# Storing an inverse transform in 16 stores of 128 partitions instead of 64 of 32, and loading the output weights in one load instead of four

## The chip, the cores and the metric

The kernel runs on one core of one Trainium2 chip. The metric is device time in microseconds (us) of one execution. The core has five engines with a queue each: PE (TensorE, matrix products into PSUM), DVE (VectorE), ACT (ScalarE), POOL (GpSimd) and SP (SyncE, which here only issues transfers). Transfers (DMAs) are issued from the SP or the POOL queue and are carried out by 16 DMA engines that the queues share.

## The reference

Two independent blocks work on 2048 positions and 640 channels each, and their results are concatenated along the channels.

- Block A is local attention with 32 heads of 20: `qkv = x @ wqkv`, each position attends to itself and 7 earlier ones (8 offsets, two apart), softmax over the 8, a weighted sum of v, then `@ wo` (640 x 640).
- Block B is a state-space convolution: a kernel K of length 2048 for each channel is summed from 192 complex exponentials, u is convolved with K through an FFT of length 4096, and `u * Dskip` is added.

```
o = einsum("bhsw,bhswd->bhsd", softmax(logits), v gathered at 8 offsets);  a = o @ wo
y = irfft(rfft(u, 4096) * rfft(K, 4096))[:2048];  b = y + u * Dskip
out = concat([a, b], axis=-1)            # (1, 2048, 1280), bf16
```

## The kernel before, in words

Everything is in bf16 with sums in PSUM. The first 270 us compute K for the five channel groups, the forward transforms, the products and the first half of the inverse transform (its results, Z, go to HBM, tensors `Zmdram` and `Zldram`), beside the projections of block A. The last 65 us, which the change touches, mix three streams:

- the weighted sum of v (`av_step`, 716): one DVE product per offset (tile `prod2` or a part of `atp`, six buffers in a ring, 714), then 16 matrix products with the identity that add it into PSUM (`ps_o`); after the eighth offset ACT copies `ps_o` into the tile `o`;
- the output product (`out_piece`, 744): five products `ps_op` of `o` and the weights `wo`, a copy into one of six `ob` rows, and a store of 128 rows of 1280 bytes;
- the second half of the inverse (`Inverse.part`, 791): 24 pieces, three for each q of 0 to 7 (blocks 0 to 2, 3 to 5 and 6 to 7 of eight). A piece is 8 or 12 matrix products of the constant table `HB` and a Z tile into `ps_ib`, and an ACT copy into the tile `ysb` (800). `ysb` has four buffers, one for each q modulo 4 (792), so the pieces of q = 4 reuse the buffer of q = 0.

When blocks 0 to 3 (half 0) or 4 to 7 (half 1) of a q are in `ysb`, they are stored: four stores of 32 partitions each, two from SP and two from POOL, 32 rows of 1280 bytes each (803, 804). Below, "store 1/0" is half 0 of q = 1. An ACT copy into a reused buffer must wait until the stores that read the blocks it overwrites have landed: the copy of blocks 3 to 5 of q = 4 waits for stores 0/0 and 0/1, the copy of blocks 0 to 2 of q = 5 waits for store 1/0.

The Z tiles are loaded by `load` (779): for q = 2 and 3 the tile lies in `LPC` and is loaded from SP by five loads of 384 KB, each of which follows the one before; for q = 6 and 7 it is loaded from POOL (and its last fifth from SP). The output weights (`open_out`, 704) are loaded from POOL into `wo`, whose place was that of the v weights until then, by four loads of 32 partitions.

The order of all instructions was worked out in advance. `Plan` (854) records each instruction, or each run of products into one PSUM tile, as a numbered group, and `issue` (889) issues the groups as the written list `ORDER` says and keeps that order on each engine. So ACT, PE, DVE and both DMA queues work strictly in order: one that waits holds up all behind it. The framework gives each DMA of the POOL queue one of eight semaphores in turn, and each DMA of the SP queue one of eight others; a DMA is issued only when the one before it on its semaphore has landed.

One more helper matters for the prediction: `hold` (391) writes the convolution table in stores from 128 partitions, whose side in HBM has an outer dimension of 8 over rows that do not join up:

```
400  dst = Kd[:, start + 256 * b:start + 256 * b + 256].rearrange("i (r s) x -> i r (s x)", s=16)
401  nc.sync.dma_start(out=dst, in_=Kh[:, b0 + b].rearrange("p s x -> p (s x)"))
```

Of the kernel before, what the change touches and what calls it, by code (L numbers as in the profile page):

```python
# [287 lines left out]
def small_half(tc, pools, co, R4, TA, TX, h):  # L288
# [22 lines left out]
    for part, sl in zip(Q, (slice(0, 16), slice(16, 48))):  # L311
        TT(part[:, 0:3:2], bc(RB[:, :, sl], 1, 2), trig[:, :, :, sl], A.mult)
# [209 lines left out]
class Attention:  # L522
# [181 lines left out]
    def open_out(self, a2):  # L704
        nc = self.nc
        self.o = a2.tile([128, 5, S], bf16, name="o")
        self.o4 = self.o[:].rearrange("p j (s i) -> p j s i", s=4)
        self.wo = self.ta.tile([128, 5, D], bf16, name="wo", tag="TX")
        wsrc = self.A_wo.rearrange("(h j dd) e -> dd h j e", j=5, dd=4)
        for dd in range(4):  # L710
            nc.gpsimd.dma_start(out=self.wo[32 * dd:32 * dd + 32], in_=wsrc[dd])
        self.ob = self.ta.tile([128, 6, D], bf16, name="ob", tag="cT")
        ring = self.ta.tile([128, 4, 2048], bf16, name="prod2", tag="R0")
        self.ring = [self.AP_[:, 2], self.AP_[:, 3]] + [ring[:, i] for i in range(4)]
# [51 lines left out]
class Inverse:  # L766
# [24 lines left out]
    def part(self, q, b0, n):  # L791
        nc = self.nc
        ysb = self.ysbs[:, q % 4]
        ps = self.att.one("ps_ib")
        for i in range(n):
            grp, g = divmod(b0 + i, 4)
            for x in range(4):
                l = 8 * q + 4 * grp + x
                self.att.MM(ps[32 * x:32 * x + 32, 160 * i:160 * i + 160], lhsT=self.HB[:, l, :], rhs=self.t[q // 2][:, g, :, l % 16, :], start=(i == 0), stop=True, skip_group_check=True, tile_position=(0, 32 * x))
        nc.scalar.copy(out=ysb[:, b0:b0 + n].rearrange("p b (t c u) -> p b c t u", c=NCH, u=4), in_=ps[:, 0:160 * n].rearrange("p (b c t u) -> p b c t u", b=n, c=NCH, u=4))  # L800
        if b0 > 0:
            grp = b0 // 6
            for x in range(4):
                (nc.sync, nc.gpsimd)[x % 2].dma_start(out=self.dst[2 * q + grp, x], in_=ysb[32 * x:32 * x + 32, 4 * grp:4 * grp + 4].rearrange("p b e -> p (b e)"))

    def parts(self):
        return [(lambda q=q, b=b, n=n: self.part(q, b, n)) for q in range(8) for b, n in ((0, 3), (3, 3), (6, 2))]
# [124 lines left out]
1086 1091-1092 1087 1155 1175 1093 1096 1149 1098 1156 1097 1151 1099 1165 1150 1147 1152-1153 1148 1178 1154 1166 1210 1170-1171 1239 1157 1186 1163 1158 1196  # L932
1195 1173 1172 1159 1182 1164 1161 1183-1185 1225 1197 1160 1240 1199 1211 1162 1198 1190 1200-1201 1212 1226 1180 1213 1176 1216 1181 1202 1189 1177 1191-1194
1229-1230 1278-1279 1222-1223 1290 1203 1217 1247 1204-1205 1291 1250-1251 1254 1233 1214 1234 1227 1215 1206 1220 1228 1260 1255 1207 1252 1265 1274 1253 1221
1261 1248 1275 1238 1271 1237 1262 1235-1236 1266 1249 1299 1276 1272 1300 1258 1273 1246 1244 1243 1280 1277 1245 1259 1224 1242 1263-1264 1256-1257 1285
1281-1283 1358 1356 1296 1359 1269-1270 1267 1357 1306 1284 1360 1303 1307 1312 1373 1315 1374 1286 1268 1308 1347 1297 1317 1304 1313 1316 1298 1305 1314 1348
1301 1326 1302 1318 1334 1310 1335 1340 1349 1352 1319 1332 1351 1350 1311 1323 1426 1294 1333 1321-1322 1292 1338-1339 1353 1361 1336 1325 1328 1354 1295
1367-1368 1345 1324 1425 1337 1309 1375 1372 1287 1376 1329 1320 1369 1547 1371 1535 1327 1377-1378 1364 1330 1341 1331 1548 1342 1379 1346 1362 1343 1370 1365
1553 1423 1393 1380 1536 1293 1355 1363 1366 1344 1382 1549 1551 1567 1550 1407 1381 1552 1554 1384 1395 1422 1383 1396 1568 1394 1288 1561 1424 1533 1427 1562
1397 1408 1398 1534 1409-1412 1571 1570 1437 1569 1564 1537-1539 1413 1566 1445 1563 1540 1430 1565 1414 1572 1421 1428 1446 1438 1429 1439 1463 1468 1454 1289  # L940
1464-1465 1460 1455 1451 1440 1466-1467 1457 1452 1441-1442 1475 1447-1448 1453 1477 1456 1476 1431 1443 1473 1478-1479 1449 1458 1432 1461 1469 1444 1450 1415
1471 1481 1474 1459 1385 1416 1480 1484 1433 1462 1436 1386 1482 1489 1435 1434 1506 1487 1490 1485 1628 1495 1488 1470 1483 1491 1629 1486 1405 1472 1503 1498
1406 1419-1420 1509 1519 1499 1417-1418 1492 1511 1510 1520 1609 1514 1512-1513 1493-1494 1497 1505 1610 1496 1504 1507 1527 1508 1516 1515 1622 1541 1518 1521
1544 1623 1528 1530 1526 1529 1522-1523 1626 1631 1517 1573 1624-1625 1558 1632 1627 1531 1542 1532 1543 1524 1545-1546 1630 1633 1555 1387 1525 1399 1589 1556
1388 1559 1574 1557 1400 1560 1575-1577 1389 1500 1392 1600 1401 1404 1403 1390-1391 1597 1501 1402 1592 1595 1502 1598 1614 1611 1596 1639 1599 1615-1616 1578
1640 1582 1619 1617-1618 1579 1588 1583 1591 1594 1602 1590 1593 1601 1634 1612 1620 1613 1621 1603 1637 1642 1604-1608 1580 1636 1638 1635 1644 1581 1643 1641
1649 1646-1647 1584-1587 1645 1650 1664 1648 1669 1651 1665 1657 1670 1667 1658 1652 1668 1671 1654 1653 1659 1655-1656 1662 1660-1661 1663 1666
"""


# [6 lines left out]
def body(tc, pools, prm, B_u, B_Dskip, Sd, Zds, Kd, LPd, A_x, A_wqkv, A_wo, out_a, out_b):  # L957
# [50 lines left out]
    def half_table(c, h, part):  # L1008
        made = trig_half(tc, pools, B, c, h, part)
        trig[c, h] = made if part == "TA" else (trig[c, h][0], made[1])  # L1010
# [240 lines left out]
```

## Time and profile before

| | |
|---|---|
| time, median of 3 runs | 368.22 us (367.98 to 368.53) |
| time of the profiled execution | 364.96 us |
| its span, first to last instruction | 363.2 us |
| granted PE clock, mean of the span | 0.911 |
| busy: PE, DVE, ACT, POOL | 297.8, 305.2, 275.9, 56.8 us |
| DMA traffic, mean over the span | 159 GB/s |

The profiled execution took 3.26 us less than the median of the three runs without a profile; 1.8 us of its time lie outside the span. In the rows of the profile, start and duration come first, in us, then the engine and what it did as `out<-in`, then in brackets how long the engine had been idle and what ended that. All instructions show line L895, since `issue` records them all there; so one goes by tiles, not by lines. "SPq" is the SP queue issuing; the number beside it is the time to issue, not to land. In a table of windows the columns are the length, the busy time and count of PE, of weight loads, DVE, ACT and POOL, then the granted PE clock, the mean busy share of the 16 DMA engines (a little over 1 where packets overlap) and what they moved.

### The profile page before, as it was taken

The page shows a single profiled execution, that of the slowest core. Times are in us where ns is not written, and L with a number is a line of the kernel's source. Part 1 is how long each engine was busy: PE and PEld are TensorE (multiplying, and loading weights), DVE is VectorE, ACT ScalarE, POOL GpSimd, SP SyncE. Part 2 cuts the span into 40 slices and gives each one's busy share as a digit, 9 for nine tenths or more (in the row PEclk, how much of TensorE's full clock was granted, in tenths as well). Part 3 has the DMA queues.
Part 4 walks back from the last instruction along what each step waited for, and adds up shares of the span by engine and source line. Part 5 has one row for each costly group of instructions (what it writes and reads, how often), then busy time and mean ns, then how long its engine had stood idle before and what let it go on. Part 6 is the DMA issues. An engine that isn't in the chain of part 4 may idle for free.

```text
span 363.2 us, 15210 instructions
## 1 busy us (share of the span) xinstructions
PE 297.8 (82%) x6737; PEld 209.4 (58%) x6747; DVE 305.2 (84%) x435; ACT 275.9 (76%) x427; POOL 56.8 (16%) x109
## 2 busy tenths in 40 slices
PE   1076886774697779788699999999999998699996
PEld 1034584533586469685376567947758764265654
DVE  5995999998899999834971997489999999689992
ACT  2999899999789999999576745938948636456752
POOL 8433200000001000000000011000002005533550
PEclk9997697698579879989899999999999999579999
DMA  6788222337646623669995375764511969993333
GB/s 143 194 226 256 57 56 52 114 115 212 176 148 155 191 63 68 209 129 219 219 184 190 81 186 154 201 243 152 205 64 40 254 189 256 264 230 111 98 120 115
DMA packets 88385, 57.57 MB, mean 159 GB/s; under 512 B 60576, under 2 KB 80480, under 8 KB 88192
## 3 DMA queue, kind: packets, MB, share of 16 engines
q1 hardware_dynamic: 83616, 44.91, 47.0%
q0 software_dynamic: 4256, 11.57, 11.6%
q8 instruction: 53, 0.87, 1.0%
q10 hardware_dynamic: 448, 0.13, 0.1%
q14 instruction: 12, 0.10, 0.1%
HBM read 27.58 MB, written 20.06 MB: 131 GB/s over the span
## 4 chain that ended last, share of the span: by engine, by line
PE 49%; ACT 10%; DVE 10%; DMA 7%; SPq 5%; issue 3%; POOL 0%; ACTq 0%; DVEq 0%
PE ps_k L895 10%; PE ps_f L895 10%; PE ps_q L895 6%; PE ps_v L895 6%; PE ps_ia L895 6%; SPq L895 5%; ACT A L895 3%; DVE prod L895 3%; PE ps_l L895 3%; PE ps_op L895 2%; PE ps_o L895 2%; ACT R L895 2%; ACT Sg L895 2%; PE ps_ph L895 2%; DMA wo<-in_A_wo_dram 2%
## 5 line engine op out<-in xcount | busy, mean ns | idle before, releaser
L895 DVE TENSOR_TENSOR Y<-G,F 128x768 bf16<-128x768 bf16 (+1 forms) x48 | 54.0, 1150 | 19.6 <-PE ps_k L895 19.6
L895 PE MATMUL ps_ph<-LPC 128*64 128x512 bf16 (+5 forms) x210 | 44.1, 412 | 20.7 <-DMA LPC<-mid 10.9
L895 ACT CAST Sg<-ps_f 128x1024 bf16<-128x1024 f32 x40 | 38.6, 1043 | 3.3 <-PE ps_f L895 3.3
L895 PEld LDWEIGHTS <-LPC 128*128 128x128 bf16 (+1 forms) x220 | 18.8, 120 | 38.7 <-issue 20.5
L895 ACT CAST A<-ps_f 128x1024 bf16<-128x1024 f32 x40 | 39.5, 1031 | 1.4 <-PE ps_f L895 1.1
L895 ACT ACTIVATE R<-LPC 128x192 bf16<-128x192 f32 (+1 forms) x105 | 36.9, 429 | 2.5 <-DVE X L895 2.3
L895 DVE TENSOR_TENSOR prod<-v,atp 128x2048 bf16<-128x2048 bf16 (+2 forms) x32 | 31.4, 1018 | 3.2 <-PE ps_o L895 3.2
L895 PEld LDWEIGHTS <-X 128*32 128x32 bf16 x1920 | 22.8, 112 | 15.4 <-issue 7.5
L895 ACT ACT_TABLE_LOAD x21 | 26.9, 1283 | 4.8 <-DMA ldt<-in_B_log_dt_dram 4.5
L895 PE MATMUL ps_k<-Y,X 128*32 128x40 bf16 x1536 | 22.4, 212 | 9.0 <-DVE X L895 3.8
L895 PE MATMUL ps_f<-A,T 128*128 128x128 bf16 x320 | 24.0, 224 | 6.0 <-ACT Sg L895 2.2
L895 ACT ACTIVATE TA<-ps_ph 128x896 bf16<-128x896 int16 x30 | 26.3, 938 | 2.8 <-PE ps_ph L895 2.7
L895 PEld LDWEIGHTS <-wv 128*32 128x32 bf16 x720 | 22.7, 120 | 7.7 <-issue 0.6
L895 DVE TENSOR_TENSOR prod<-wq,LPC 128x5120 bf16<-128x5120 bf16 (+1 forms) x11 | 20.1, 1849 | 7.2 <-ACT LPC L895 7.2
L895 DVE TENSOR_TENSOR X<-R,TX 128x768 bf16<-128x768 bf16 x40 | 21.0, 556 | 6.1 <-ACT TX L895 3.2
L895 PEld LDWEIGHTS <-T 128*128 128x128 bf16 x320 | 19.7, 100 | 9.5 <-issue 8.0
L895 PE MATMUL ps_op<-wo,o 128*128 128x320 bf16 x160 | 24.2, 302 | 0.2
L895 DVE TENSOR_TENSOR prod<-qT,LPC 128x1024 bf16<-128x1024 bf16 (+1 forms) x16 | 23.1, 1486 | 0.8 <-PE ps_l L895 0.8
L895 PE MATMUL ps_v<-xT,wv 128*32 128x512 bf16 x400 | 23.5, 380 | 0.0
L895 PE MATMUL ps_q<-xT,wq 128*128 128x512 bf16 x100 | 22.8, 379 | 0.0
L895 PE MATMUL ps_k<-xT,wk 128*128 128x512 bf16 x100 | 22.7, 379 | 0.0
L895 POOL DMA_DIRECT2D out_dram<-ysb x32 | 16.2, 511 | 36.2 <-ACT ysb L895 33.3
(129 smaller groups left out, 623.8 us busy)
## 6 DMA issues: line engine op xcount, KB each, us to landing
Zmdram<-Z SPq DMA_DIRECT2D x16, 256.0 KB
Xp<-X SPq DMA_DIRECT2D x20, 192.0 KB
Sdram<-Sg SPq DMA_DIRECT2D x12, 256.0 KB
P<-Sdram SPq DMA_DIRECT2D x6, 512.0 KB
P<-Sdram SPq DMA_DIRECT2D x12, 256.0 KB
Z<-Zmdram POOLq DMA_DIRECT2D x8, 384.0 KB, 6.5
U<-in_B_u_dram SPq DMA_DIRECT2D x4, 640.0 KB
Ksb<-Kdram SPq DMA_DIRECT2D x20, 128.0 KB
```

Of the source, the lines that this page charges most:

```text
L895: ins = getattr(getattr(self.tc.nc, engine), method)(*map(real, a), **{n: real(x) for n, x in k.items()})
```

## The change

In `Inverse.part` the four stores of a half become one store from 128 partitions; half 0 goes from SP and half 1 from POOL. In `open_out` the four loads of `wo` become one load into 128 partitions from POOL. Bytes and layout in HBM stay as they are. On the HBM side a store is now 4 x 32 rows of 640 values, where the outer 4 steps by one position and the 32 by 64 positions; the load of `wo` reads 4 x 160 rows of 640 values. On the SBUF side both have 128 partitions.

```
-        for dd in range(4):
-            nc.gpsimd.dma_start(out=self.wo[32 * dd:32 * dd + 32], in_=wsrc[dd])
+        nc.gpsimd.dma_start(out=self.wo[:], in_=wsrc)
...
             grp = b0 // 6
-            for x in range(4):
-                (nc.sync, nc.gpsimd)[x % 2].dma_start(out=self.dst[2 * q + grp, x], in_=ysb[32 * x:32 * x + 32, 4 * grp:4 * grp + 4].rearrange("p b e -> p (b e)"))
+            (nc.sync, nc.gpsimd)[grp].dma_start(out=self.dst[2 * q + grp], in_=ysb[:, 4 * grp:4 * grp + 4].rearrange("p b e -> p (b e)"))
```

There are 51 groups less (1672 before), so `ORDER` is renumbered. All other groups keep their order. Each store stands where the last of its four stood, and the load of `wo` where the third of its four stood.

More of the change, by code (lines that the diff above doesn't have):

```diff
@@ L934 @@
 1229-1230 1278-1279 1222-1223 1290 1203 1217 1247 1204-1205 1291 1250-1251 1254 1233 1214 1234 1227 1215 1206 1220 1228 1260 1255 1207 1252 1265 1274 1253 1221
-1261 1248 1275 1238 1271 1237 1262 1235-1236 1266 1249 1299 1276 1272 1300 1258 1273 1246 1244 1243 1280 1277 1245 1259 1224 1242 1263-1264 1256-1257 1285
-1281-1283 1358 1356 1296 1359 1269-1270 1267 1357 1306 1284 1360 1303 1307 1312 1373 1315 1374 1286 1268 1308 1347 1297 1317 1304 1313 1316 1298 1305 1314 1348
-1301 1326 1302 1318 1334 1310 1335 1340 1349 1352 1319 1332 1351 1350 1311 1323 1426 1294 1333 1321-1322 1292 1338-1339 1353 1361 1336 1325 1328 1354 1295
@@ L938 @@
[L938 to L945, printed above, removed]
@@ L946 @@
-1640 1582 1619 1617-1618 1579 1588 1583 1591 1594 1602 1590 1593 1601 1634 1612 1620 1613 1621 1603 1637 1642 1604-1608 1580 1636 1638 1635 1644 1581 1643 1641
-1649 1646-1647 1584-1587 1645 1650 1664 1648 1669 1651 1665 1657 1670 1667 1658 1652 1668 1671 1654 1653 1659 1655-1656 1662 1660-1661 1663 1666
+1261 1248 1275 1238 1271 1237 1262 1235-1236 1266 1249 1296 1276 1272 1297 1258 1273 1246 1244 1243 1280 1277 1245 1259 1224 1242 1263-1264 1256-1257 1285
+1281-1283 1349 1347 1293 1350 1269-1270 1267 1348 1303 1284 1351 1300 1304 1309 1361 1312 1362 1286 1268 1305 1341 1294 1314 1301 1310 1313 1295 1302 1311 1342
@@ new lines @@
+1298 1323 1299 1315 1331 1307 1332 1334 1316 1329 1343 1308 1320 1402 1330 1318-1319 1344 1352 1322 1325 1345 1292 1358-1359 1339 1321 1401 1333 1306 1287 1326
+1317 1517 1508 1324 1363 1355 1327 1335 1328 1518 1336 1364 1340 1353 1337 1360 1356 1520 1399 1375 1365 1509 1346 1354 1357 1338 1367 1531 1386 1366 1519 1521
+1369 1377 1398 1368 1378 1532 1376 1288 1528 1400 1506 1403 1529 1379 1387 1380 1507 1388-1391 1410 1392 1418 1510 1406 1530 1393 1533 1397 1404 1419 1411 1405
+1412 1436 1441 1427 1289 1437-1438 1433 1428 1424 1413 1439-1440 1430 1425 1414-1415 1448 1420-1421 1426 1450 1429 1449 1407 1416 1446 1451-1452 1422 1431 1408
@@ new lines @@
+1434 1442 1417 1423 1394 1444 1454 1447 1432 1370 1395 1453 1457 1435 1371 1455 1462 1409 1479 1460 1463 1458 1580 1468 1461 1443 1456 1464 1581 1459 1384 1445
+1476 1471 1385 1482 1492 1472 1396 1465 1484 1483 1493 1564 1487 1485-1486 1466-1467 1470 1478 1565 1469 1477 1480 1500 1481 1489 1488 1577 1511 1491 1494 1514
+1578 1501 1503 1499 1502 1495-1496 1490 1534 1525 1579 1504 1512 1505 1513 1497 1515-1516 1582 1522 1372 1498 1381 1547 1523 1373 1526 1535 1524 1382 1527
+1536-1538 1473 1558 1374 1555 1474 1383 1550 1553 1475 1556 1569 1566 1554 1588 1557 1570-1571 1539 1589 1543 1574 1572-1573 1540 1546 1544 1549 1552 1560 1548
@@ L948 @@
+1551 1559 1583 1567 1575 1568 1576 1561 1586 1591 1562-1563 1541 1585 1587 1584 1593 1542 1592 1590 1598 1595-1596 1545 1594 1599 1613 1597 1618 1600 1614 1606
+1619 1616 1607 1601 1617 1620 1603 1602 1608 1604-1605 1611 1609-1610 1612 1615
 """
```

## Prediction

> **What bounds the kernel now.** I first cut the span into stages by a table of windows.
>
> ```profile
> core 0: us, PE busy (x) PEld busy (x) DVE busy (x) ACT busy (x) POOL busy (x), PEclk, DMA share, GB/s
> 302.00:321.90 19.90, 14.46 (x347) 7.33 (x346) 14.95 (x16) 11.16 (x18) 12.42 (x23) 0.67 1.07 255
> 321.90:352.70 30.80, 29.91 (x751) 18.11 (x750) 30.27 (x31) 19.07 (x40) 13.23 (x26) 0.99 0.41 126
> 316.00:320.00 4.00, 3.74 (x107) 1.79 (x108) 2.53 (x3) 2.08 (x5) 2.20 (x5) 0.50 1.05 232
> ```
>
> From 302 to 321.9 no compute engine is full, but the DMA share is 1.07: all 16 DMA engines are busy without a pause, at 255 GB/s, 15.9 GB/s each. From 321.9 to 352.7 DVE is busy 30.27 of 30.8 us, and the last output products follow it. So whatever moves the start of the second stage moves the end, and a transfer that lands late in the first stage has no slack to hide in. At 316 to 320 PE has half its clock.
>
> Then the instructions of that first stage in order of time, ACT, PE and DVE:
>
> ```profile
> 314.69 0.56 ACT L895 CAST ysb<-ps_ib 128x480 bf16<-128x480 f32 x1 [3.51 <-DMA out_dram<-ysb]
> 315.15 1.02 ACT L895 CAST o<-ps_o 128x1024 bf16<-128x1024 f32 x1
> 316.06 0.50 PE L895 MATMUL ps_o<-prod,ident 32*32 32x384 bf16 x2 [3.38 <-issue]
> 317.62 0.89 ACT L895 CAST ysb<-ps_ib 128x480 bf16<-128x480 f32 x2 [1.45 <-PE ps_o L895]
> 318.23 0.99 PE L895 MATMUL ps_ib<-Z,HB 96*32 96x160 bf16 x24 [0.20 <-ACT ysb L895]
> 321.90 1.76 DVE L895 RECIPROCAL recip<-ps_s 128x256 bf16<-128x256 f32 x1 [1.74 <-PE ps_s L895]
> ```
>
> ACT at 314.69 copies a piece of q = 4 and waits 3.51 us for a store. Behind it in ACT's queue stands the copy of `o` that frees PSUM for PE, so PE stands 3.38 us. At 317.62 ACT copies q = 5 and needs store 1/0; the row names PE, but the chain of waits shows the store landing just then, at 312.25 + 5.14 = 317.39:
>
> ```profile
> 304.94 7.03 DMA wo<-in_A_wo_dram
> 311.97 0.28 issue
> 312.25 5.14 DMA out_dram<-ysb
> ...
> 320.05 1.82 PE ps_s L895 x8
> ```
>
> The POOL queue says why the store went out so late:
>
> ```profile
> 311.31 0.50 POOL L895 DMA_DIRECT2D out_dram<-ysb  x1 [1.96 <-DMA wo<-in_A_wo_dram]
> 312.25 0.50 POOL L895 DMA_DIRECT2D out_dram<-ysb  x1 [0.44 <-DMA wo<-in_A_wo_dram]
> 312.74 0.70 POOL L895 DMA_DIRECT2D Z<-Zmdram  x1
> 313.44 0.61 POOL L895 DMA_DIRECT2D wo<-in_A_wo_dram  x1
> ```
>
> Each of the two waits is for the DMA eight places earlier in its queue: the semaphores have come round to loads of `wo` that have not landed.
>
> **What goes.** With one DMA in place of four on each half, and one load of `wo`, eight semaphores reach back far enough, and the 1.96 + 0.44 us go. At best all of PE's standing goes, 3.38 + 0.20 = 3.6 us: that caps the gain. Issuing gets cheaper on both queues, but neither queue is itself on the path; I count 0.
>
> **What a store of 128 partitions costs.** No row shows the new form, so I bound it by two that are near: the store of `ob` (128 partitions, HBM side one dimension of 128 rows) and the store of the convolution table (128 partitions, HBM side 8 x 16 rows). First their issue in the SP queue, then a window in the data of each, two for the table:
>
> ```profile
> 77.89 1.81 SPq L895 DMA_DIRECT2D Kdram<-Kl  x3
> 359.17 1.65 SPq L895 DMA_DIRECT2D out_dram<-ob  x3
> ```
>
> ```profile
> 79.30:79.45 0.15, 0.15 (x29) 0.15 (x28) 0.15 (x1) 0.15 (x1) 0.00 (x0) 1.00 0.54 160
> 157.70:157.90 0.20, 0.20 (x8) 0.20 (x8) 0.20 (x1) 0.20 (x2) 0.00 (x0) 0.50 0.54 159
> 360.20:360.40 0.20, 0.00 (x0) 0.00 (x0) 0.00 (x0) 0.20 (x1) 0.00 (x0) 1.00 1.00 358
> ```
>
> The store of `ob` fills the DMA engines (1.00, 358 GB/s, 22.4 GB/s each); the table's store with its outer 8 never gets past 0.54, half of them. So the outer dimension on the HBM side limits how many engines share a DMA. The new stores and the new load of `wo` have an outer 4: between 4 engines of 16 (share 0.25) and all 16. The table's store is the nearer row; I take **4 engines**. A store of 163,840 bytes then puts 41 KB on each of 4 engines in place of 10.2 KB on each of 16: quiet, 1.83 us of data instead of 0.46; in the full stage at 15.9 GB/s, 2.6 instead of 0.64.
>
> By the Trainium skill, page "DMA: Bandwidth & Descriptors", section "Why a DMA increments its semaphore by 16 and not by 1", the number of engines is the largest one up to 16 that divides the outer sizes of both sides, on the POOL queue too save for some direct copies that get 16: this gives the 4 that I take, and the exception is a rival below.
>
> **The sum, on the time of the profiled execution (364.96 us).**
>
> (a) Store 1/0, which the copy at 317.62 needs. I take it that SP's stores always fall on the same 4 engines, and `wo` on 4 others. By its landing one of SP's engines has moved, against before: two SP stores more (0/0 and 1/0), 2 x (41 - 10) = +61 KB; store 0/1 from POOL, if it meets them, 0 to +31, say +15; no `wo`, three of whose four loads had gone (3 x 204,800 / 16), -38; no store 1/1, -10; half of a POOL load of 393,216 bytes that was held till 312.74 and now isn't, +12. Net +40 KB, at 15.9 GB/s +2.5 us. Against this, the engines without stores run dry early, and the last third of the 12 us from 305.5 to 317.4 then goes at nearer 22 than 16 GB/s: -1.0. And no quarter of the store is held back till 312.25: -0.5. **+1.0 us**, bounds -1.5 (the two reliefs twice as large, no 0/1) and +3.
>
> (b) `wo`: 204,800 bytes on each of 4 engines.
>
> ```profile
> wk<-in_A_wqkv_dram POOLq DMA_DIRECT2D x1, 800.0 KB, 5.0
> wo<-in_A_wo_dram POOLq DMA_DIRECT2D x4, 200.0 KB, 6.7
> 112.00:115.00 3.00, 2.27 (x30) 1.78 (x28) 3.00 (x9) 3.00 (x4) 0.00 (x0) 1.00 0.86 283
> 307.42 0.55 SPq L895 DMA_DIRECT2D LPC<-Zmdram  x1
> 316.16 0.55 SPq L895 DMA_DIRECT2D LPC<-Zmdram  x1
> 322.44 0.56 SPq L895 DMA_DIRECT2D LPC<-Zldram  x1
> DMA to landing us min/median/max: 5.4/6.6/7.7
> 328.50 0.32 PE L895 MATMUL ps_ib<-LPC,HB 96*32 96x160 bf16 x8
> 321.66 1.21 PE L895 MATMUL ps_op<-wo,o 128*128 128x320 bf16 x5
> ```
>
> At 15.9 to 17.7 GB/s (the load of `wk`, 283 / 16) this is 11.6 to 12.9 us of data from about 305.5, so `wo` lands at 318 to 321, before its first use at 321.66: hidden, with a us to spare. But a Z load spreads over all engines and is as late as its slowest. On the four with `wo` the third Z load of `LPC` lies beside 205 KB of `wo`, a POOL load and another of SP: 280 KB at 17 GB/s, 16 us, till 318 to 321, where its successor was issued at 316.16 before. The last of the chain then goes out at 324 to 327 instead of 322.44; a load of this size (the "to landing" row is of POOL's Z loads from 290 to 330 us) lands 5.4 us after issue at the least, so at 330 to 332 at worst, and PE wants it at 328.50 plus what (a) costs. Between 0 and +2.4; the chain speeds up once the stage empties, so **+0.6**.
>
> (c) Stores 3/0 to 2/1 in the second stage. Most copies come late enough, but not the one that reuses store 3/1:
>
> ```profile
> 331.69 1.02 POOL L895 DMA_DIRECT2D out_dram<-ysb  x2 [1.83 <-ACT ysb L895]
> 334.22 0.42 ACT L895 CAST ysb<-ps_ib 128x320 bf16<-128x320 f32 x1 [0.37 <-PE ps_ib L895]
> 334.54 0.81 ACT L895 CAST o<-ps_o 128x768 bf16<-128x768 f32 x1
> DMA to landing us min/median/max: 1.8/4.0/7.4
> DMA to landing us min/median/max: 2.1/2.2/3.6
> ```
>
> The last two rows are POOL's stores of `ysb` and of `ob`. The second quarter went out at 332.20 and landed 1.8 later, 334.0: no slack. One store on 4 engines lands 2.1 + 1.83 - 0.46 = 3.5 us after 331.69, at 335.2, 1.0 late. Queued behind the copy is that of `o`, then PE's next products; DVE's ring of six takes up part. 0 to +0.9, **+0.4**.
>
> (d) What is pushed out of the slow-clock stretch runs faster: the 1.82 us of `ps_s` ran at half clock, and some of it passes 322: **-0.2**. The rest (tail, `ob` stores on all engines) stays.
>
> Sum +1.0 + 0.6 + 0.4 - 0.2 = +1.8: 366.8 on the profile's base. The three runs' median is 368.22, so **370.0 us**, own range 368.4 to 372.
>
> **Rivals.**
>
> 1. *Faster: the stores spread over all 16 engines.* Then the semaphore waits are simply gone. `wo` into 128 partitions moves like `wk`, 283 GB/s, where 32-partition loads of it ran at 215:
>
> ```profile
> 307.00:309.00 2.00, 1.24 (x29) 0.53 (x30) 2.00 (x3) 1.05 (x1) 1.49 (x4) 0.94 1.09 215
> ```
>
> That is 0.9 us less on 51 KB an engine, against 25 KB more in front of store 1/0 (1.6 us). It decides by whether store 1/0 lands before 317.4; by 314 all 3.6 us are won. Half of the cap, with the last quarter no longer held back, gives -1.7: 366.5 (364.6 to 367.9). For it: the whole stall hangs on two late POOL stores. Against it: the 0.54 of the table's store. 0.23. The Trainium skill's same page ("Rules for kernel authors") speaks for it: one 128-partition transfer in place of several on parts of the partitions, since these share the same engines anyway.
>
> 2. *Only SP's stores are narrow, POOL's are wide* (the exception named above would give this). Each SP engine has 61 + 13 + 12 = 86 KB more, +5.4 us, less 1.5 for the others running dry, 0.5 for the quarter and 0.9 for the quicker `wo`: +2.5, no (b), no (c), -0.2: 370.5. 0.18.
>
> 3. *`wo` falls on the same four engines as SP's stores.* +167 KB there, at up to 22 GB/s 7.6 us, of which some is hidden behind what is counted in (a): +6, 374. No row shows where a POOL DMA begins. 0.12.
>
> 4. *The wait only changes hands:* store 1/0 lands within 0.7 us of 317.4 and the Z chain holds: 368.2. 0.05.
>
> **How the numbers follow.** Forecast 0.42, rivals 0.23, 0.18, 0.12, 0.05. A measurement of this kernel can tell about 0.2% (0.7 us) from no change. Faster by more: 0.21 of rival 1, 0.02 each of the low ends of the forecast and of rival 2, together 0.25. Within: rival 4's 0.05, 0.02 of rival 1, 0.03 of the forecast, 0.10. Slower: the rest, 0.65. The range 366.0 to 373.0 takes in the forecast, rivals 2 and 4 and the nearer half of rival 1; it leaves out rival 3 and the deep end of rival 1, some 0.2.
>
> **What would show it.** (a) a window inside a lone SP store of `ysb` (after 335) with a DMA share near 0.25, not 1.00; no POOL wait for a `wo` load; ACT's copy of q = 5 at 318 to 320. (b) the Z loads of `LPC` from SP farther apart, and PE waiting before its first `ps_ib<-LPC`. (c) ACT idle about 1 us before a `ysb` copy near 335. Wrong it is if those windows show 1.00, or if the copy of q = 5 starts before 317: then the wide stores win, and PE's 3.38 us are gone.

## The result, and the profile after

The changed kernel takes 380.42 us (median of 4 runs, 377.66 to 382.15) against 368.38 us (367.98 to 368.71) of the kernel before in the same comparison: a ratio of 1.032, interval 1.0254 to 1.0387. It is slower by some 12 us; the forecast was 1.8 us slower. The profiled execution took 377.66 us, the shortest of the four, and its span is 375.9. Executions over 1.5% above the fastest of the same kernel are left out of all ratios below (six of z_last's twelve, at most three of any other), and the profiled ones of wo_late and z_last are among them, so the table gives no lengths for these two.

To see where the 12.7 us of span come from I cut both traces at the same three instructions: ACT's copy of blocks 3 to 5 of q = 0, DVE's RECIPROCAL, and the last copy of `o`. The two rows of before that the prediction does not show (the RECIPROCAL is there, at 321.90), and before's window from the first to the second:

```profile
302.39 0.56 ACT L895 CAST ysb<-ps_ib 128x480 bf16<-128x480 f32 x1 [0.27 <-PE ps_ib L895]
352.70 1.22 DVE L895 CAST o<-ps_o 128x1024 bf16<-128x1024 f32 x1 [0.53 <-PE ps_o L895]
```

```profile
302.39:321.90 19.51, 14.07 (x333) 6.95 (x326) 14.56 (x16) 11.04 (x17) 12.42 (x23) 0.66 1.07 255
```

The same three in the changed kernel (all its lines are L893), and its windows between them, with two shorter ones; columns as in the prediction:

```profile
301.74 0.56 ACT L893 CAST ysb<-ps_ib 128x480 bf16<-128x480 f32 x1 [0.27 <-PE ps_ib L893]
330.51 1.76 DVE L893 RECIPROCAL recip<-ps_s 128x256 bf16<-128x256 f32 x1 [9.61 <-PE ps_s L893]
365.21 1.22 DVE L893 CAST o<-ps_o 128x1024 bf16<-128x1024 f32 x1 [0.66 <-PE ps_o L893]
```

```profile
301.74:330.51 28.77, 14.77 (x333) 7.31 (x326) 14.84 (x16) 11.15 (x17) 7.56 (x9) 0.60 0.81 185
330.51:365.21 34.70, 30.45 (x751) 18.42 (x750) 30.58 (x32) 18.90 (x40) 7.69 (x13) 0.98 0.33 102
322.00:326.00 4.00, 0.59 (x12) 0.37 (x12) 0.00 (x0) 0.56 (x1) 0.00 (x0) 0.50 0.33 100
349.60:350.20 0.60, 0.60 (x49) 0.42 (x42) 0.00 (x0) 0.10 (x1) 0.21 (x1) 1.00 0.26 98
```

The first stage grew from 19.51 to 28.77 us (+9.26), the second from 30.80 to 34.70 (+3.9), the tail by 0.2; the 300 us ahead were 0.65 us shorter. The work of the first stage is nearly the same (PE 14.77 us against 14.07, DVE 14.84 against 14.56), so the growth is standing. The DMA engines are no longer full: 0.81 and 185 GB/s where before had 1.07 and 255. From 322 to 326 a third of them is busy and PE works 0.59 of 4 us: a few DMA engines have all that is left to move, and the compute engines stand. The last row lies inside a lone store of `ysb`: a share of 0.26, that is 4 engines of 16.

ACT and PE in the first stage, then ACT in the second:

```profile
311.88 0.56 ACT L893 CAST ysb<-ps_ib 128x480 bf16<-128x480 f32 x1
323.30 0.56 ACT L893 CAST ysb<-ps_ib 128x480 bf16<-128x480 f32 x1 [9.94 <-DMA out_dram<-ysb]
326.77 0.89 ACT L893 CAST ysb<-ps_ib 128x320 bf16<-128x320 f32 x2 [2.92 <-DMA out_dram<-ysb]
346.07 0.43 ACT L893 CAST ysb<-ps_ib 128x320 bf16<-128x320 f32 x1 [2.86 <-DMA out_dram<-ysb]
351.57 0.56 ACT L893 CAST ysb<-ps_ib 128x480 bf16<-128x480 f32 x1 [1.87 <-DMA out_dram<-ysb]
```

```profile
316.80 0.50 PE L893 MATMUL ps_o<-prod,ident 32*32 32x384 bf16 x2 [3.48 <-issue]
323.91 0.59 PE L893 MATMUL ps_ib<-Z,HB 96*32 96x160 bf16 x12 [5.13 <-ACT ysb L893]
327.25 0.59 PE L893 MATMUL ps_ib<-Z,HB 96*32 96x160 bf16 x12 [2.75 <-ACT ysb L893]
```

The copy of q = 4 (311.88) no longer waits for a store. The copy of q = 5, blocks 0 to 2 (323.30) waits 9.94 us for store 1/0, whose last post came at 323.20; the copy of blocks 6 and 7 (326.77) waits another 2.92 for store 1/1. A post is one DMA engine's count on the semaphore of a DMA; with its last post a DMA has landed. PE stands behind them, 5.13 and 2.75 us. The DMA queues say how old those stores are, POOL first, then SP, then the groups of DMAs with their median time to landing:

```profile
303.31 1.99 POOL L893 DMA_DIRECT2D wo<-in_A_wo_dram  x1
306.32 0.71 POOL L893 DMA_DIRECT2D out_dram<-ysb  x1 [0.34 <-ACT ysb L893]
```

```profile
306.95 0.56 SPq L893 DMA_DIRECT2D LPC<-Zmdram  x1
307.61 0.68 SPq L893 DMA_DIRECT2D out_dram<-ysb  x1
325.74 0.56 SPq L893 DMA_DIRECT2D LPC<-Zmdram  x1
331.35 0.60 SPq L893 DMA_DIRECT2D LPC<-Zldram  x1
```

```profile
Z<-Zmdram POOLq DMA_DIRECT2D x8, 384.0 KB, 11.5
wo<-in_A_wo_dram POOLq DMA_DIRECT2D x1, 800.0 KB, 22.3
```

Store 1/0 left SP at 307.61 and was 15.6 us old when the copy could start; store 1/1 left POOL at 306.32, 3 us behind `wo`, and was 20.4 us old. `wo` took 22.3 us, till 325.61. The load of `LPC` that went out at 316.16 before goes out at 325.74. No POOL wait for `wo` is left, as the change intended: the 2.4 us of semaphore waits are gone, and longer landings have come in their place.

### The profile page after: what moved, and what is told of

It reads as the page before. It is cut to its first block, busy times and chain, and to the rows that moved or that the text cites. A ratio compares the mean times of both kernels' runs of the same rounds, so it can differ in the third digit from the quotient of the medians.

```text
span 375.9 us, 15133 instructions
## 1 busy us (share of the span) xinstructions
PE 294.7 (78%) x6737; PEld 207.3 (55%) x6747; DVE 305.1 (81%) x435; ACT 275.9 (73%) x427; POOL 46.8 (12%) x82
## 4 chain that ended last, share of the span: by engine, by line
PE 40%; ACT 19%; issue 13%; DVE 5%; DMA 3%; SPq 2%; POOL 2%; ACTq 0%; POOLq 0%; DVEq 0%
PE ps_f L893 9%; PE ps_k L893 7%; PE ps_v L893 6%; PE ps_q L893 5%; PE ps_ia L893 5%; ACT Sg L893 4%; ACT R L893 4%; ACT L893 3%; ACT A L893 3%; PE ps_l L893 3%; SPq L893 2%; ACT TA L893 2%; POOL out_dram L893 2%; PE ps_op L893 2%; ACT TX L893 2%
## 5 line engine op out<-in xcount | busy, mean ns | idle before, releaser
L893 DVE TENSOR_TENSOR Y<-G,F 128x768 bf16<-128x768 bf16 (+1 forms) x48 | 54.0, 1150 | 19.9 <-PE ps_k L893 19.9
L893 PE MATMUL ps_ph<-LPC 128*64 128x512 bf16 (+5 forms) x210 | 41.1, 385 | 18.9 <-DMA LPC<-mid 10.5
L893 ACT CAST Sg<-ps_f 128x1024 bf16<-128x1024 f32 x40 | 38.6, 1040 | 3.2 <-PE ps_f L893 3.1
L893 ACT CAST A<-ps_f 128x1024 bf16<-128x1024 f32 x40 | 39.4, 1024 | 1.4 <-PE ps_f L893 1.1
L893 ACT ACTIVATE R<-LPC 128x192 bf16<-128x192 f32 (+1 forms) x105 | 36.9, 429 | 2.2 <-DVE X L893 2.0
L893 DVE TENSOR_TENSOR prod<-v,atp 128x2048 bf16<-128x2048 bf16 (+2 forms) x32 | 31.5, 1019 | 7.3 <-PE ps_o L893 7.3
L893 PEld LDWEIGHTS <-LPC 128*128 128x128 bf16 (+1 forms) x220 | 17.7, 114 | 35.0 <-issue 16.3
L893 PEld LDWEIGHTS <-X 128*32 128x32 bf16 x1920 | 22.8, 112 | 17.7 <-DVE X L893 7.9
L893 PE MATMUL ps_k<-Y,X 128*32 128x40 bf16 x1536 | 22.6, 213 | 11.6 <-issue 4.2
L893 ACT CAST ysb<-ps_ib 128x480 bf16<-128x480 f32 (+1 forms) x24 | 12.1, 518 | 23.1 <-DMA out_dram<-ysb 19.4
L893 PE MATMUL ps_f<-A,T 128*128 128x128 bf16 x320 | 23.9, 224 | 6.2 <-ACT Sg L893 2.5
L893 ACT ACTIVATE TA<-ps_ph 128x896 bf16<-128x896 int16 x30 | 26.1, 938 | 1.6 <-DVE F L893 0.8
L893 PEld LDWEIGHTS <-wv 128*32 128x32 bf16 x720 | 22.9, 120 | 7.8 <-issue 1.0
L893 PE MATMUL ps_op<-wo,o 128*128 128x320 bf16 x160 | 24.5, 304 | 3.3 <-ACT ysb L893 3.1
L893 DVE TENSOR_TENSOR prod<-wq,LPC 128x5120 bf16<-128x5120 bf16 (+1 forms) x11 | 20.1, 1849 | 7.3 <-ACT LPC L893 7.3
L893 PEld LDWEIGHTS <-T 128*128 128x128 bf16 x320 | 19.5, 100 | 9.5 <-issue 7.7
L893 DVE TENSOR_TENSOR X<-R,TX 128x768 bf16<-128x768 bf16 x40 | 20.7, 553 | 4.7 <-ACT TX L893 2.5
L893 DVE TENSOR_TENSOR prod<-qT,LPC 128x1024 bf16<-128x1024 bf16 (+1 forms) x16 | 23.1, 1485 | 0.9 <-PE ps_l L893 0.9
L893 PE MATMUL ps_v<-xT,wv 128*32 128x512 bf16 x400 | 23.6, 381 | 0.0
L893 PE MATMUL ps_q<-xT,wq 128*128 128x512 bf16 x100 | 22.8, 379 | 0.0
L893 PE MATMUL ps_k<-xT,wk 128*128 128x512 bf16 x100 | 22.7, 379 | 0.0
```

The lines of the kernel that those rows point to most:

```text
L893: ins = getattr(getattr(self.tc.nc, engine), method)(*map(real, a), **{n: real(x) for n, x in k.items()})
```

## The experiments

Each ratio is against runs of the kernel before on the same chip. "First" is the length from the copy at 302.39 to RECIPROCAL, "second" from there to the last copy of `o`, in the profiled execution; lengths are compared and not starts, since the copy starts at 301.7 to 308.6 us in these executions. One execution of each kernel was profiled; wo_alone (below), which is the kernel before up to its end, has 19.32 and 30.70, and so shows how well a length repeats.

| kernel | ratio, interval | first | second |
|---|---|---|---|
| before | 1 | 19.51 | 30.80 |
| changed | 1.0320 (1.0254 to 1.0387) | 28.77 | 34.70 |
| stores_only | 1.0236 (1.0170 to 1.0302) | 23.47 | 36.17 |
| wo_only | 1.0323 (1.0242 to 1.0404) | 29.80 | 30.89 |
| both_wide | 1.0010 (0.9969 to 1.0051) | 19.13 | 31.55 |
| stores_wide | 1.0316 (1.0239 to 1.0394) | 28.70 | 31.36 |
| wo_behind | 1.0374 (1.0327 to 1.0421) | 20.39 | 42.21 |
| eight_engines | 1.0105 (1.0064 to 1.0145) | 24.23 | 32.06 |
| late_stores | 1.0092 (1.0059 to 1.0124) | 18.93 | 34.00 |
| wo_late | 0.9977 (0.9940 to 1.0014) | | |
| wo_z_late | 1.0004 (0.9966 to 1.0043) | 16.37 | 33.52 |
| z_last | 0.9989 (0.9939 to 1.0038) | | |
| z_last_lpc | 0.9953 (0.9915 to 0.9990) | 16.78 | 33.49 |
| z_split | 0.9917 (0.9882 to 0.9952) | 16.30 | 30.70 |
| wide_late | 0.9943 (0.9904 to 0.9982) | 17.68 | 30.96 |

### Each part alone

stores_only takes the change of the stores and leaves the four loads of `wo`; wo_only is the reverse.

```
 stores_only: (nc.sync, nc.gpsimd)[grp].dma_start(out=self.dst[2 * q + grp], in_=ysb[:, 4 * grp:4 * grp + 4]...)
 wo_only:     nc.gpsimd.dma_start(out=self.wo[:], in_=wsrc)
```

> One part alone: the 16 merged stores of the changed kernel, the output weights by four loads as in the kernel before. Three theories of the 12 us by which the changed kernel is slower. A: the one load of wo, which ran 22.3 us in the changed kernel and in that time held back the DMAs of the POOL queue behind it and the slices of the Z loads on the same engines, cost the 8.8 us of the first stage, and the merged stores cost the 3.9 us after it; then this kernel takes 371 to 373 us and RECIPROCAL starts at 321 to 323. B: the stores themselves cost it, since store 1/0 landed only 15.6 us after its issue; then 378 to 380, RECIPROCAL near 330. C: each alone is harmless and only the two together fill an engine; then 368 to 370.

> The other part alone: 64 stores of 32 partitions as before, wo by one load of 128 partitions. A: the load still runs some 20 us and the POOL stores and Z loads behind it land with it, so 375 to 377 us, RECIPROCAL at 328 to 330, the rest of the kernel as before. B: 368 to 370. C: 368 to 370, with the cost in neither part alone.

wo_only's time is as theory A has it (376.82 us); stores_only's (374.40) is more than A allowed and less than B. Their RECIPROCAL, at 338.37 and 328.29, comes later than A had it, but 6.2 and 2.4 us of these starts lie ahead of the copy. Each part alone costs most of the 12 us. From the copy on, wo_only loses in the first stage alone (+10.3); the second is as before. There the stores are in 32-partition pieces on all engines, but stand behind `wo` (ACT, then the DMA group):

```profile
332.61 0.56 ACT L894 CAST ysb<-ps_ib 128x480 bf16<-128x480 f32 x1 [15.25 <-DMA out_dram<-ysb]
```

```profile
wo<-in_A_wo_dram POOLq DMA_DIRECT2D x1, 800.0 KB, 19.5
```

In stores_only the first stage grows by 3.96 us and the second by 5.37. Two stores hold the first stage, 0/0 and then 1/0, the one of the forecast (SP, ACT, PE):

```profile
307.21 0.62 SPq L894 DMA_DIRECT2D out_dram<-ysb  x1
310.26 0.59 SPq L894 DMA_DIRECT2D out_dram<-ysb  x1
328.99 0.59 SPq L894 DMA_DIRECT2D LPC<-Zldram  x1
```

```profile
321.38 0.56 ACT L894 CAST ysb<-ps_ib 128x480 bf16<-128x480 f32 x1 [7.86 <-DMA out_dram<-ysb]
324.02 0.89 ACT L894 CAST ysb<-ps_ib 128x480 bf16<-128x480 f32 x2 [1.16 <-DMA out_dram<-ysb]
```

```profile
337.85 0.32 PE L894 MATMUL ps_ib<-LPC,HB 96*32 96x160 bf16 x8 [2.74 <-DMA LPC<-Zldram]
```

Store 0/0 is 14.1 us old when the copy of q = 4 may overwrite its blocks; store 1/0 lands at 323.92, 13.7 us old, and the copy of q = 5 follows it at 324.02. In the second stage PE waits 2.74 us for the last load of `LPC`. This load went out about as soon after RECIPROCAL as in before (0.7 us against 0.5), but it took 8.7 us to land against 4.5: twelve of its sixteen slices had landed after 4.3 us, and the last four came after 5.7 to 8.7, behind the two narrow stores of q = 4 and 5 that SP had issued ahead of it. The parts do not add up (first stages +3.96 and +10.29 alone, +9.26 together): ACT waits for whichever store lands last.

### The number of engines

Against the changed kernel, both_wide and stores_wide change addresses in HBM alone, eight_engines takes an outer dimension of 8:

```
 both_wide:     out=self.rows[2 * q + grp]      # rows = out_b.rearrange("(k p) c -> k p c", p=128)
                in_=self.A_wo.rearrange("(j p) e -> p j e", p=128)
 stores_wide:   the stores of both_wide, wo from wsrc
 eight_engines: rows = out_b.rearrange("(b k a) c -> k a b c", a=8, b=16)
                in_=self.A_wo.rearrange("(b j a) e -> a b j e", a=8, b=16)
```

> As the changed kernel in all but the addresses in HBM: each store writes 128 rows that follow one another, and wo is read as 128 rows that follow one another for each of the five parts, so the outer dimension in HBM is 128 and not 4. Sizes of the pieces (1280 bytes), bytes, order and waits are the same; the rows of block B come out in another order and block A is multiplied by weights with their rows exchanged. If the number of engines that share a DMA is what costs the 12 us (A and B alike), the stores of ysb fill the DMA engines (share near 1.00), the wait for wo is gone, and it takes 365 to 368 us, below the kernel before. The rival: that a DMA of 160 or 800 KB is large, and waits behind it last longer, whatever the number of engines; then 372 or more.

> As the run before it, but wo is read as in the changed kernel, with the outer 4: merged stores over rows that follow one another (the rows of block B come out in another order), wo on few engines. A: the stage from 302 us on is as in the changed kernel, 375 to 377 us, and the 3.9 us of the second stage are gone. B: 366 to 369 us. C: 366 to 370.

> As both_wide, but the outer dimension in HBM is 8 in the stores and in the load of wo (rows of block B in another order, rows of the weights exchanged). If the outer dimension gives the number of engines, a store fills half of them (DMA share near 0.5 inside a lone store of ysb), wo puts 102 KB on each of 8 engines and lands some 12 us after its issue, before its first use, and the time lies between the two others: 1.00 to 1.012 of the kernel before, near 1.005. If it takes 1.025 or more, few engines are not the cause but the shape with an outer dimension; if 8 engines are as good as 16 (within 0.002), the cost of few engines sets in between 4 and 8.

With 16 engines the 12 us are gone, with 8 a third is left (and `wo` lands after 16.3 us, where 12 were expected). Windows inside a lone store of `ysb`, both_wide first, then eight_engines:

```profile
333.40:333.80 0.40, 0.40 (x5) 0.20 (x2) 0.40 (x1) 0.36 (x1) 0.00 (x0) 1.00 0.98 410
```

```profile
343.90:344.30 0.40, 0.40 (x30) 0.33 (x35) 0.32 (x1) 0.00 (x0) 0.15 (x1) 1.00 0.50 186
```

Shares of 0.98, 0.50 and (changed kernel) 0.26: the outer dimension in HBM sets the number of engines. The rows of these kernels also lie elsewhere in HBM, which no run changes by itself; but a busy engine moves nearly the same in all three, 25.6, 23.3 and 24.5 GB/s (410 / 16, 186 / 8, 98 / 4), so the places of the rows matter little. The posts say the same; in us from issue:

```
SP, lone store 3/0:  both_wide      1.58 ... 1.89                             (16 posts)
                     eight_engines  1.02 | 2.65 2.80 ... 2.93                 (1 + 8)
                     changed        0.96 | 3.65 3.69 3.71 3.78                (1 + 4)
POOL, wo, changed:   6.18 ... 10.94 (12 posts) | 19.62 21.26 22.20 22.30      (16 posts)
POOL, store 1/1:     5.80 ... 10.97 (12 posts) | 18.26 19.32 20.35 20.37      (16 posts)
```

A lone store takes 1.9, 2.9 and 3.8 us on 16, 8 and 4 engines. From SP only the engines with data post, besides one post that comes some 1 us after the issue, ahead of all data; from POOL all 16 post, and behind `wo` four posts of every DMA come late, as those of `wo` do. The Trainium skill says this in "DMA: Bandwidth & Descriptors", section "Why a DMA increments its semaphore by 16 and not by 1": on the POOL queue all 16 engines post whatever the shape, and 4 and 8 are the divisors it gives; the trace agrees on both.

stores_wide shows that a wide store is no help beside a narrow `wo` (SP, ACT):

```profile
309.11 1.02 SPq L894 DMA_DIRECT2D out_dram<-ysb  x1
```

```profile
328.34 0.89 ACT L894 CAST ysb<-ps_ib 128x480 bf16<-128x480 f32 x2 [14.25 <-DMA out_dram<-ysb]
```

Store 1/0 goes from the other queue, over 16 engines, and is still 19 us old: four of its posts come after 18.3 to 19.1 us, the other twelve by 10.7, so the slices on the four engines of `wo` come last. Its second stage is near before's (31.36), which leaves most of the 3.9 us of the changed kernel to the narrow stores.

### What the order of POOL's queue does

```
 changed:   store 0/1, wo, Z, store 1/1, Z, ...
 wo_behind: store 0/1, Z, store 1/1, wo, Z, ...
```

> The changed kernel with one instruction moved: the one load of wo is issued from POOL just behind store 1/1, some 3 us later than in the changed kernel, in place of ahead of it. Theory A, a POOL DMA cannot complete before the one ahead of it in its queue has: store 1/1 now lands at 311 to 316 us in place of 326.7, ACT's copy of blocks 6 and 7 of q = 5 follows the copy of blocks 0 to 2 at once, and the time falls by about 3 us against the changed kernel, to 1.020 to 1.028 of the kernel before; wo itself is late instead and lands at 326 to 330. Rival D, the engines are shared and the order in the queue does not matter: store 1/1 lands past 320 all the same and the ratio stays at 1.03.

The local part of theory A holds and the total does not (POOL, ACT, PE):

```profile
307.76 0.71 POOL L893 DMA_DIRECT2D out_dram<-ysb  x1 [2.33 <-ACT ysb L893]
```

```profile
319.29 0.89 ACT L893 CAST ysb<-ps_ib 128x480 bf16<-128x480 f32 x2 [3.09 <-DMA out_dram<-ysb]
```

```profile
328.80 1.51 PE L893 MATMUL ps_op<-wo,o 128*128 128x320 bf16 x5 [5.26 <-DMA wo<-in_A_wo_dram]
```

Ahead of `wo`, store 1/1 lands in 7.4 us in place of 20.4, both copies of q = 5 go from 319.29 on, right behind store 1/0 (landed at 319.19), and the first stage is 20.39 us, 0.9 over before. But `wo` again needs 20.3 us, now till 328.75, and PE waits for it, with DVE and its ring behind. The 8 us only changed hands, and the ratio is 1.0374 where theory A had 1.020 to 1.028.

### Two terms by themselves

```
 late_stores: if q % 4 >= 2: one store of 128 partitions;  else: the four of before
 wo_alone:    kernel before, and at its end
              att.nc.gpsimd.dma_start(out=att.wo[:], in_=A_wo.rearrange("(h j dd) e -> dd h j e", j=5, dd=4))
              att.nc.gpsimd.dma_start(out=att.wo[:], in_=A_wo.rearrange("(j p) e -> p j e", p=128))
```

> Only the stores of q = 2, 3, 6 and 7, which leave after the crowded stage, are merged (8 stores of 128 partitions for 32); all else is as in the kernel before. It tests the term (c) of the forecast alone. By the forecast, one narrow store lands 3.5 us after its issue and only the copy that needs store 3/1 is 1.0 us late: 1.000 to 1.003 of before. If in a quiet stage a narrow store costs about twice what the forecast gave it (in the changed kernel three copies waited 2.86, 1.87 and 1.78 us for stores 4 to 6 us old), 1.006 to 1.012. If most of the second stage's 3.9 us was a backlog from the first, near 1.000.

> The kernel before, and at its very end, with almost nothing else in flight, the weights wo are loaded twice more: first as in the changed kernel (outer 4 in HBM), then over rows that follow one another. If four engines carry the first, at the 22.4 GB/s of an engine that the store of ob shows, it lands 9.1 us of data plus about 2 after its issue, 11 us; the second 4 to 5. If the first takes 18 us or more even alone, the 22 us in the changed kernel are the DMA's own and not the crowd's; if some 11, about half of the 22 us was waiting for the other traffic of those engines.

late_stores costs 0.9%, as its second expectation has it, and 3.2 us in the second stage, so most of the 3.9 us there are the narrow stores' own. ACT waits for three of them, 2.49 (below), 0.95 and 1.12 us:

```profile
340.57 0.42 ACT L898 CAST ysb<-ps_ib 128x320 bf16<-128x320 f32 x1 [2.49 <-DMA out_dram<-ysb]
```

wo_alone, POOL's two loads, then windows in the data of each:

```profile
359.35 2.02 POOL L895 DMA_DIRECT2D wo<-in_A_wo_dram  x1 [4.87 <-PE ps_op L895]
375.38 0.88 POOL L895 DMA_DIRECT2D wo<-in_A_wo_dram  x1 [14.01 <-DMA wo<-in_A_wo_dram]
```

```profile
366.00:372.00 6.00, 0.00 (x0) 0.00 (x0) 0.00 (x0) 0.00 (x0) 0.00 (x0) 0.50 0.25 78
378.00:380.00 2.00, 0.00 (x0) 0.00 (x0) 0.00 (x0) 0.00 (x0) 0.00 (x0) 0.50 0.88 346
```

In this one execution the narrow load takes 15.7 us even alone, the wide one 5.4: 819 KB at 78 GB/s are 10.5 us, the rest is issue and start. Neither expectation fits. If the start is alike in the crowd, then of the 22.3 us in the changed kernel 15.7 are the load's own and 6.6 the crowd's.

### Where the gain of the removed waits went

both_wide has no wait for `wo` on POOL either, and wins nothing. Its first stage:

```profile
302.62:321.75 19.13, 14.59 (x333) 7.34 (x326) 14.74 (x16) 11.05 (x17) 5.84 (x9) 0.61 1.05 275
```

```profile
315.38 0.50 PE L894 MATMUL ps_o<-prod,ident 32*32 32x384 bf16 x2 [1.57 <-issue]
318.08 0.99 PE L894 MATMUL ps_ib<-Z,HB 96*32 96x160 bf16 x24 [0.73 <-ACT ysb L894]
```

```profile
307.79 0.56 SPq L894 DMA_DIRECT2D out_dram<-ysb  x1
317.47 0.89 ACT L894 CAST ysb<-ps_ib 128x480 bf16<-128x480 f32 x2 [2.48 <-PE ps_o L894]
```

The DMA engines are as full as before (1.05). Store 1/0 now goes out at 307.79, where its last quarter had been held till 312.25, but its last post comes at 317.37, just ahead of the copy at 317.47: 14.75 us behind the first copy, where before has 15.00. So the wait for a semaphore went and the store landed no sooner. PE's 3.38 + 0.20 us of standing became 1.57 + 0.73, but PE was busy 14.59 us in place of 14.07, at a granted clock of 0.61 in place of 0.66. So I left the DMAs as in before and changed only what is issued ahead of what:

```
POOL, before:     stores 0, wo x3 among them, Z, stores 1, Z, wo, stores 4/1, Z, Z, stores 5 and 4/0
POOL, wo_late:    stores 0, Z, stores 1, wo x3, Z, wo, stores 4/1, Z, Z, ...
POOL, wo_z_late:  stores 0, stores 1, wo x4, stores 4/1, Z x4, stores 5 and 4/0
POOL, z_last:     stores 0, stores 1, wo x4, stores 4/1, stores 5 and 4/0, Z x4
z_last_lpc:       z_last, and SP's last load of LPC ahead of the stores of q = 4 and 5
z_split:          z_last_lpc, but stores 4/1, Z x2, stores 5 and 4/0, Z x2
wide_late:        the order of z_split with the DMAs of both_wide
```

> The kernel before, all DMAs as they are, with one change of order: three of the four loads of wo go out from POOL behind the stores of q = 0 and q = 1, and no longer between them. If the stores that ACT waits for were late because loads of wo lay ahead of them in POOL's queue and its semaphores, PE's 3.38 us of standing shrink to 1 or less and the time falls by 1 to 3 us, 0.992 to 0.997 of before. If the DMA engines are full either way and only the sum of the bytes counts (the merged stores on 16 engines took the semaphore waits away and won nothing), it stays within 0.002.

> As wo_late, and two of POOL's Z loads, which PE needs only past 330 us, go out behind the stores of q = 4's second half too, so 0.8 MB less lies ahead of the stores that ACT waits for. If bytes ahead of those stores are what counts, the stall goes, 0.988 to 0.995 of before. If not, or if the Z loads come late in turn, 0.998 to 1.005.

> As wo_z_late, but all four of POOL's Z loads go out behind the stores of q = 4 and 5. wo_z_late won 3.1 us up to RECIPROCAL and gave back 2.7 after it, because the last load of LPC landed beside the Z loads, with PE waiting for it. If that collision is what gave it back, the Z loads now leave LPC room and 0.990 to 0.996 of before is left; rival: the Z loads themselves are now too late for q = 7, and it stays at 0.998 to 1.004.

> As z_last, and SP issues the last load of LPC right behind the one before it, ahead of the stores of q = 4 and 5. If LPC bounds the start of the second stage, 0.988 to 0.994 of before; if the stores behind that load delay the copies that reuse their buffers, or Z is late, 0.997 or more.

> As z_last_lpc, but two of POOL's four Z loads go out ahead of the stores of q = 5 and two behind them, so that store 3/1 no longer queues behind four Z loads (ACT waited 1.85 us for it). If that wait is worth its length, 0.987 to 0.994 of before; if the two early Z loads delay the loads of LPC as in wo_z_late, 0.996 to 1.001.

> The order of z_split with the DMAs of both_wide: merged stores and one load of wo, all over rows that follow one another, so on 16 engines (rows of block B in another order, rows of the weights exchanged); wo goes out behind the stores of q = 1. If merging is worth something once the Z loads are out of the way, 0.005 below z_split or more; if it is worth nothing either way, within 0.003 of it.

wo_late and z_last cannot be told from no change. wo_z_late wins 3.14 us in the first stage and gives 2.72 back in the second. There PE waits for the last load of `LPC`: the row (PE) names no cause, but the load's last post comes at 328.36, 7.3 us after its issue where before has 4.5, and it runs beside the last three of four Z loads. z_last_lpc sends that load earlier and is the first whose interval lies below 1 (0.9953, between its two expectations), with store 3/1 late behind the Z loads (ACT):

```profile
328.45 0.32 PE L895 MATMUL ps_ib<-LPC,HB 96*32 96x160 bf16 x8 [1.88 <-issue]
```

```profile
334.92 0.42 ACT L895 CAST ysb<-ps_ib 128x320 bf16<-128x320 f32 x1 [1.85 <-DMA out_dram<-ysb]
```

z_split mends that too and keeps both stages short:

```profile
303.50:319.80 16.30, 13.94 (x333) 6.86 (x326) 14.55 (x17) 10.94 (x17) 10.86 (x21) 0.69 0.98 254
319.80:350.50 30.70, 29.79 (x751) 18.08 (x750) 30.17 (x31) 19.08 (x40) 14.64 (x28) 1.00 0.50 152
```

3.2 us less in the first stage, none given back: 364.66 us against 367.68, 0.9917, some 0.8% less than before, with the whole interval below 1. wide_late, the same order with the merged DMAs on 16 engines, is at 0.9943, within 0.003 of it. both_wide took the semaphore waits away and kept the bytes ahead of the stores, and won nothing; wo_z_late kept the DMAs and moved those bytes, and the first stage fell by 3.1 us. So the stall before was a matter of which bytes lay ahead of the stores, not of the number of DMAs. The Trainium skill, page "DMA: Bandwidth & Descriptors", section "Rules for kernel authors", advises one 128-partition transfer in place of transfers on parts of the partitions; where the outer dimension leaves 16 engines that costs nothing here (1.001) and wins nothing, and where it leaves 4 it costs 3.2%. The Trainium skill's rule a few rows on, that a dimension whose size is a multiple of 16 should stand outermost, is the one that decided.

## Why the prediction was wrong

The direction and the width were right. The size was not, 12 us in place of 1.8 and outside the range, and the path by which most of it came stands in no term. The sum had +1.4 us for the first stage, (a) + (b) + (d), and +0.4 for the second; +9.26 and +3.9 were measured. Of the 9.26, 6.33 lie ahead of the copy of q = 5 (store 1/0) and 2.93 behind it (store 1/1, behind `wo`). Point by point.

- **The bounds** held: the first stage hung on stores of `ysb`, and the waits on POOL's semaphores went. That removing them would bring up to 3.6 us was an upper bound; both_wide shows that by itself it brings nothing.
- **The width** was right: 4 engines from SP (0.26) and from POOL (0.25 in wo_alone).
- **(b), the load of `wo`, is the step that failed.** "Hidden, with a us to spare", +0.6, at most +2.4: with `wo` alone narrow the first stage is 10.3 us longer (wo_only), with `wo` narrow and the stores merged but wide 9.2 (stores_wide). Two things were missed. First, `wo` landed at 325.61 and not at 318 to 321. The sum let its data start at 305.5; alone, 5.2 of its 15.7 us are issue and start, so near 308.5 is the better estimate. From there its 205 KB an engine took some 17 us, 12 GB/s and not 15.9 to 17.7, with slices of the Z loads on the same engines. Second, it was not `wo` itself that was waited for in the changed kernel. The sum asked only when `wo` and the Z loads of `LPC` were needed, but store 1/1 stands behind `wo` in POOL's queue and landed 1.1 us after it; wo_behind, with the store ahead, shows that this, and not the store's own width, made it 20.4 us old. The chain of `LPC`, which the term did price, came later than its bound (its own 16 us from 305.5 end at 321.5, not 321, and the next load went out at 325.74), but PE, itself late by then, waited only 0.72 us for its last load:

```profile
338.18 0.32 PE L893 MATMUL ps_ib<-LPC,HB 96*32 96x160 bf16 x8 [0.72 <-DMA LPC<-Zldram]
```

- **(a), store 1/0**, +1.0 with +3 as the upper end, was mis-sized: from the copy at 302.39 to the copy of q = 5 it is 15.23 us before, 19.20 in stores_only and 21.56 in the changed kernel, +4.0 and +6.3 (the copy went at 323.30, where 318 to 320 had been named as the sign). In both kernels store 1/0 came last for this copy, as the term has it. A part of it can be read from the posts of the changed kernel: two Z loads of POOL, issued at 316.59 and 317.29 before, went out at 313.42 and 314.11, and twelve of the sixteen slices of the first had landed by 323.11, ahead of store 1/0's last post at 323.20. That is at least 25 KB an engine that the sum does not have. How much POOL's stores put on SP's engines no run tells, so whether the bytes or the 15.9 GB/s were further off stays open.
- **(c), the second stage**, +0.4: late_stores measures +3.2. The latency of a lone narrow store was nearly right (3.5; measured 3.8 on SP, 4.5 to 4.9 on POOL). The failing part is "most copies come late enough, but not the one": three copies come too early, not one (in the changed kernel they wait 2.86, 1.87 and 1.78 us). It also left out that a Z load behind narrow stores is late on their engines, which cost PE 2.74 us in stores_only.
- **(d)** had the wrong sign: the stage at the low clock grew, and its mean clock was 0.60 in place of 0.66.
- **The rivals.** Wide stores (1): refuted by 0.26, and both_wide shows that the rival's -1.7 would not have come either. Only SP narrow (2): refuted, POOL's are narrow too. The same four engines for `wo` and SP's stores (3): the four last slices of the load of `LPC` issued at 306.95 land at 323.7 to 325.7 like those of `wo`, while store 1/0, behind it in the same queue, landed whole by 323.2; so its four are others. That is read from the posts, not tried in a run. The wait changing hands (4) at no cost: refuted by the 12 us.

I had priced `wo` by when its own data is needed. What it cost was the landing of the DMAs around it.

## What to carry to other kernels

Before merging DMAs, look at the outermost dimension on both sides: with 4, four engines carried it all here, and a window inside one lone DMA with a share of 0.26 shows it. Price such a DMA not only by its own due time but by the one behind it in its queue and by every DMA that has a slice on its engines. In this stage, with its DMA engines full, a wait on a store was mended by issuing later what is needed later (z_split, 0.9917), not by fewer DMAs (both_wide, 1.001).

## What the runs showed of the hardware that I had not expected

- A narrow load of 800 KB took 15.7 us alone on 4 engines against 5.4 on 16, and POOL needed 2.0 us to issue it against 0.9. Its engines moved 19.5 GB/s each, so more than 5 us of the 15.7 went into issue and start.
- A DMA spread over all 16 engines, from another queue, was 19 us old when it landed: twelve of its posts had come by 10.7 us, the last four came at 327.4 to 328.2, right behind the last four of `wo` (325.8 to 326.6; stores_wide).
- On POOL a DMA has 16 posts of engines even where 4 have data, and behind `wo` the last four of each came late; on SP only the engines with data post, four or eight. Whether store 1/1 had its data on the four engines of `wo` or only its posts, no run tells.
